# Pooled attention, MLP and experts on one core: weight work in the bursts, high parts of k on GpSimd, transposes around the bursts

## The chip, the cores and the metric

The kernel runs on one core of a Trainium2 chip. The metric is the device time of one execution in microseconds. TensorE (PE in the rows) multiplies matrices, VectorE (DVE) and ScalarE (ACT) work on them element by element, GpSimd (POOL) likewise, and SyncE (SP) issues most loads. Rows write L337 for line 337 of the kernel before; PEld is TensorE loading its stationary operand.

## The reference

```python
# q, k, v: (2, 8, 1152, 64)
q_pool = q.reshape(B, H, S // 2, 2, D).mean(axis=3)
scores = np.matmul(q_pool, k.transpose(0, 1, 3, 2)) / np.sqrt(D)
attn = np.exp(scores - scores.max(-1, keepdims=True))
attn = attn / (attn.sum(-1, keepdims=True) + 1e-09)
x = np.matmul(attn, v)                      # (2, 8, 576, 64) -> (1152, 512)
x = np.maximum(x @ w_in, 0.0) ** 2 @ w_out  # 512 -> 2048 -> 512
# then each token goes to the best of 8 experts, with a capacity:
# out[i] = gate[i] * (relu(x[i] @ w1[e]) @ w2[e])
```

All arrays are float32; the change touches only attention and the preparation of `w_in` and `w_out`, which arrive as 64-bit floats and are narrowed on the chip.

## The kernel before, in words

Products that need more than one pass of reduced precision are made of two parts: a high part (a rounded copy, `fp32r`) and a low part (source minus high part). This holds for q, k, the attention's output x, and the MLP's weights.

**Attention.** A pair is two heads of one batch; there are eight, `p` = 0 to 7. A pair has nine score tiles, so 72 steps: the tile of step n is n itself, the tiles of pair p are 9p to 9p+8. Eight tiles hold 128 pooled queries of one head; the ninth (`h` is None) holds the last 64 of both heads and has twice as many matmuls. `run_step(n)` writes the order of the work by hand. It has the scores of tile n in three pieces (`s_unit`, L337 with k's high part, L339 with its low part; banks sc, two sets in turn), the maximum (`s_max`, VectorE, L344), the exponential (`s_exp`, ScalarE, L349), and the sum's reciprocal of the tile before (`s_rec`, VectorE, L357, L358). Older tiles are transposed (`t_unit`, L372) in three groups: group 0 of tile n-2 into bank bm, copied by ScalarE (L380); group 1 of tile n-2 into bank ba, copied by VectorE (L379), with the reciprocal as its fourth block; group 2 of tile n-3 into the spare columns of the score banks, copied by ScalarE (L380, `late`).

After its tiles are transposed, a pair's tiles meet v in bursts (`burst`, L397): at step 9p+7 the first (u = 0, bank ba), at step 9p+12, which is step 3 of the next pair, the tail (u = 2, bank bm) and then the second (u = 1, bank ba). Behind a burst VectorE scales its two halves (L403), ScalarE makes the high part of x (L407) and GpSimd the low part (L408). In a burst step the order is: scores, maximum, exponential, `late`, reciprocal, burst, extra work, group 0, group 1. In another step: scores, maximum, half of the extra work, group 0, group 1, exponential, `late`, reciprocal, the other half. An engine takes its instructions in this order.

Extra work hangs on steps by `at(n, f)`. The next pair's q halves are added by GpSimd (`q_sum`, L294), scaled by ScalarE (`q_piece`, L299), and the low part is made by VectorE (`q_low`, L304, with a small copy by GpSimd, L308). k comes in three pieces of 384 columns: high part on ScalarE (`k_piece`, L318), low part on GpSimd (L321; for the first pair on VectorE). The first head of a pair does this in the pair's steps 3 to 5, the second in steps 6 to 8 (one later for the first pair), then the loads for the pair after go out on SyncE's queue. On SyncE too are the clearing of two DRAM arrays, the loads of v after each second burst, and those of the MLP's weights.

Five of the sixteen weight blocks of the MLP are prepared in attention, in the order in 0, out 0, in 1, out 1, in 2. A block is loaded and then narrowed by three VectorE instructions of 128x1024 (L169, L175, L181; `narrow_ops` gives the load and the three), at steps 6 to 20, 28 to 36, 39 to 47 and 50 to 58. It is then split: high part on GpSimd (L201, the first two) or ScalarE (L199, the other three), low part on VectorE (L205).

**After attention** follow the MLP, with TensorE matmuls L754 and L780, the choice of experts and the experts' matmuls. The MLP's first matmul follows the last burst.

**Start.** The loads of the first pair go out on SyncE's queue in the order q (first head, 256 columns), k (first head, three pieces), q and k (second head), the rest of q, v. Each load of k is two instructions, one for either half of the partitions.

Of the kernel before, what the change touches and what calls it, by code (L numbers as in the profile page):

```python
# [21 lines left out]
def tile_pooled_attention__relu2_mlp__top1_experts(  # L22
# [14 lines left out]
    nc = tc.nc  # L37
# [105 lines left out]
    wf = {}  # L143
# [132 lines left out]
    def load_k(p, h, c=slice(0, S), eng=nc.sync):  # L276
        b, hp = pairs[p]
        src = k[b, 2 * hp + h][:, c]
        for i in range(2):
            eng.dma_start(out=kqs[h][i * D : (i + 1) * D, c], in_=src)  # L280

    def load_qk(p, h):
        load_q(p, h)
        load_k(p, h)
# [57 lines left out]
    def s_max(n):  # L342
        nm = st[n]["nm"] = sm.tile([P, 1], F32, tag="nm", name="nm", bufs=4)
        nc.vector.tensor_reduce(out=nm, in_=st[n]["S"][:, :, :KS], axis=AX.XY, op=ALU.max, negate=True)  # L344
# [18 lines left out]
    def t_unit(n, i):  # L363
        p, h, j, z = tiles[n]
        bank = (bank_m, bank_a, None)[i]
        if i < 2:
            src = bank.rearrange("p (c n) -> p c n", n=P)
        else:
            src = bank_sets[(n + LAG[2]) % 2][:, :2, KS:]
        for m, c in enumerate(TG[i]):  # L370
            x = st[n]["rc"].to_broadcast([P, P]) if c is None else st[n]["P"][:, c * P : (c + 1) * P]
            nc.tensor.transpose(src[:, m, :], x, ident)  # L372
        blocks = slice(4 * i, 4 * i + len(TG[i]))
        if h is None:
            dst = ptz.rearrange("p c h n -> p c (h n)")[:, blocks, :]
        else:
            dst = pts[:, z, blocks, h, :]
        if i == 1:
            return lambda: nc.vector.tensor_copy(out=dst, in_=src)  # L379
        return lambda: nc.scalar.activation(out=dst, in_=src, func=AF.Copy)  # L380
# [30 lines left out]
        burst(p, 0)  # L411

    def burst1(p):
        burst(p, 2)
        burst(p, 1)
        if p + 1 < NPR:
            load_v(p + 1)

# [7 lines left out]
    for p in range(NPR):  # L426
        big[NT9 * p + 3 + LAG[2] + 1] = lambda p=p: burst0(p)
        big[NT9 * p + 8 + LAG[2] + 1] = lambda p=p: burst1(p)

    def run_step(n):  # L430
        extra = todo.pop(n, [])
        cut = len(extra) // 2
        old = [n - x if 0 <= n - x < N else None for x in LAG]
        late = lambda: None
        if n < N:
            s_unit(n, 0)
            s_unit(n, 1)
        if old[2] is not None:
            late = t_unit(old[2], 2)
        if n < N:  # L440
            s_unit(n, 2)
            s_max(n)
        if n in big:
            if n < N:
                s_exp(n)
            late()
            if 0 < n <= N:
                s_rec(n - 1)
            big[n]()
        for f in extra[:cut]:  # L450
            f()
        for i in range(2):
            if old[i] is not None:
                t_unit(old[i], i)()
        if n not in big:
            if n < N:
                s_exp(n)
            late()
            if 0 < n <= N:
                s_rec(n - 1)  # L460
        for f in extra[cut:]:
            f()

# [1 line left out]
    Q0 = (slice(0, 2 * P), slice(2 * P, SQ))  # L465
    load_q(0, 0, Q0[0])
    for i in range(3):
        load_k(0, 0, slice(i * KS, (i + 1) * KS))
    load_qk(0, 1)
    load_q(0, 0, Q0[1])  # L470
    load_v(0)
    one = const.tile([P, 1], F32, name="one")
# [12 lines left out]
    q_low(0, 0, Q0[0])  # L485
    for i in range(3):
        k_piece(0, 0, i)
    q_sum(1, nc.vector)
    q_piece(0, 1)
    q_low(0, 1)  # L490
    for i in range(3):
        at(0, lambda i=i: k_piece(0, 1, i))
    at(1, lambda: q_sum(0, c=Q0[1]))
    at(2, lambda: q_piece(0, 0, Q0[1]))
    at(2, lambda: q_low(0, 0, Q0[1]))
# [3 lines left out]
    for p in range(NPR - 1):  # L499
        n0 = NT9 * p  # L500
        for h in range(2):
            m = n0 + 2 + 3 * h + (p == 0)
            at(m, lambda h=h: q_sum(h))
            at(m + 1, lambda p=p, h=h: k_piece(p + 1, h, 0))
            at(m + 1, lambda p=p, h=h: q_piece(p + 1, h))
            at(m + 2, lambda p=p, h=h: q_low(p + 1, h))
            for i in (1, 2):
                at(m + 1 + i, lambda p=p, h=h, i=i: k_piece(p + 1, h, i))
            if p + 2 < NPR:
                at(m + 3, lambda p=p, h=h: load_qk(p + 2, h))  # L510

# [1 line left out]
    parts = list(clear_rows())  # L513
    for u in range(len(parts)):
        at(3 + u * 20 // len(parts), lambda: clear_some(parts, 1))
    ops = [f for _ in range(2) for f in nwork.pop(0)]
    for u, f in enumerate(ops):
        at((6, 11, 12, 13, 14, 18, 19, 20)[u], f)
    at(22, lambda: split_hi(("in", 0), wf["in", 0]))
    at(23, lambda: split_lo(("in", 0), wf["in", 0]))  # L520
    at(25, lambda: split_hi(("out", 0), wf["out", 0]))
    at(26, lambda: split_lo(("out", 0), wf["out", 0]))
    for w in range(3):
        for u, f in enumerate(nwork.pop(0)):
            at(28 + 11 * w + (0, 4, 6, 8)[u], f)
    for n, key in ((64, ("in", 1)), (67, ("out", 1)), (N + 1, ("in", 2))):
        at(n, lambda key=key: split_hi(key, wf[key], "act"))
        at(n + 1, lambda key=key: split_lo(key, wf[key]))
    for n in range(N + LAG[2] + 1):
        run_step(n)  # L530
    assert not todo
    att.close()


# [689 lines left out]
```

## Time and profile before

| | us |
|---|---|
| median of 3 runs (lowest to highest) | 663.76 (662.58 to 663.93) |
| profiled execution, its own time | 663.67 |
| its span, first to last instruction | 661.9 |
| TensorE, VectorE, ScalarE, GpSimd busy in the span | 605.4, 362.5, 276.4, 131.3 |
| mean granted clock of TensorE, as a share | 0.984 |

The span is 1.8 us shorter than the execution's time. Busy time is a sum over stages that differ: attention ends at about 299 us. A busy TensorE includes the modelled end of each matmul, which overlaps the next one, so its true idle time is larger than what is left over.

### The profile page before, as it was taken

The page shows a single profiled execution, that of the slowest core. Times are in us where ns is not written, and L with a number is a line of the kernel's source. Part 1 is how long each engine was busy: PE and PEld are TensorE (multiplying, and loading weights), DVE is VectorE, ACT ScalarE, POOL GpSimd, SP SyncE. Part 2 cuts the span into 40 slices and gives each one's busy share as a digit, 9 for nine tenths or more (in the row PEclk, how much of TensorE's full clock was granted, in tenths as well). Part 3 has the DMA queues.
Part 4 walks back from the last instruction along what each step waited for, and adds up shares of the span by engine and source line. Part 5 has one row for each costly group of instructions (what it writes and reads, how often), then busy time and mean ns, then how long its engine had stood idle before and what let it go on. Part 6 is the DMA issues. An engine that isn't in the chain of part 4 may idle for free. (4 is left out here: it accounts for less than half of the span.)

```text
span 661.9 us, 10087 instructions
## 1 busy us (share of the span) xinstructions
PE 605.4 (91%) x3873; PEld 462.5 (70%) x3873; DVE 362.5 (55%) x660; ACT 276.4 (42%) x556; POOL 131.3 (20%) x173
## 2 busy tenths in 40 slices
PE   4998898998899989999999999999999788899994
PEld 2876776777777867769899998998988434444342
DVE  4867777777796867747666688233435311111110
ACT  3765666676767676643232323222343111110110
POOL 3242416141323241001000121000201202000011
PEclk7899999999999999999999999999999989999998
DMA  7795843441625310401223348400100499299800
GB/s 192 192 279 178 261 154 91 112 126 43 189 55 158 86 37 1 164 1 65 64 75 125 119 175 283 178 1 1 40 1 18 158 352 264 94 390 356 292 8 13
DMA packets 35994, 89.23 MB, mean 135 GB/s; under 512 B 4257, under 2 KB 5157, under 8 KB 35936
## 3 DMA queue, kind: packets, MB, share of 16 engines
q1 hardware_dynamic: 34560, 85.66, 41.2%
q0 software_dynamic: 1376, 2.81, 1.2%
q8 instruction: 35, 0.57, 0.4%
q14 instruction: 23, 0.19, 0.1%
HBM read 78.55 MB, written 11.37 MB: 136 GB/s over the span
## 5 line engine op out<-in xcount | busy, mean ns | idle before, releaser
L754 PE MATMUL bs<-ar 128*128 128x384 f32 x576 | 109.0, 338 | 0.0
L344 DVE TENSOR_REDUCE nm<-sc 128x1 f32<-128x1152 f32 x72 | 97.4, 1353 | 18.7 <-PE sc L339 18.0
L754 PEld LDWEIGHTS bs<-ar 128*128 128x128 f32 x576 | 101.6, 188 | 5.0 <-issue 1.6
L349 ACT ACTIVATE af<-sc,nm 128x1152 f32<-128x1152 f32 x72 | 88.1, 1224 | 37.8 <-DVE nm L344 35.8
L337 PE MATMUL sc<-ar 128*128 128x384 f32 x240 | 91.3, 397 | 11.8 <-ACT af L380 5.5
L780 PE MATMUL bt<-ar 128*128 128x512 f32 x360 | 93.2, 395 | 1.2 <-DVE ar L766 1.2
L339 PE MATMUL sc<-ar 128*128 128x384 f32 x240 | 79.4, 347 | 1.1 <-POOL ar L321 0.4
L780 PEld LDWEIGHTS bt<-ar 128*128 128x128 f32 x360 | 66.3, 188 | 14.0 <-DVE ar L766 2.0
L760 ACT ACTIVATE af<-bs 128x384 f32<-128x384 f32 x48 | 23.6, 492 | 121.3 <-PE bs L754 118.3
L397 PE MATMUL ba<-af 128*64 128x256 f32 x576 | 65.3, 380 | 2.1 <-DVE su L357 1.9
L764 DVE TENSOR_TENSOR af<-af 128x384 f32<-128x384 f32 x48 | 26.7, 556 | 71.0 <-ACT af L760 71.0
L337 PEld LDWEIGHTS sc<-ar 128*128 128x128 f32 x240 | 45.5, 195 | 19.5 <-ACT af L380 11.9
L397 PEld LDWEIGHTS ba<-af 128*64 128x64 f32 x576 | 40.0, 137 | 22.8 <-DVE su L357 3.4
L379 DVE COPY af<-ba 128x512 f32<-128x512 f32 x72 | 49.3, 685 | 8.8 <-PE ba L372 8.1
L372 PE MATMUL ba<-ident,af 128*128 128x128 f32 x216 | 37.6, 283 | 15.6 <-DVE af L403 6.7
L380 ACT ACTIVATE af<-bm 128x512 f32<-128x512 f32 x72 | 42.9, 596 | 21.4 <-PE bm L372 21.3
L339 PEld LDWEIGHTS sc<-ar 128*128 128x128 f32 x240 | 46.4, 195 | 2.8 <-POOL ar L321 1.5
L408 POOL TENSOR_TENSOR ar<-af,ar 128x256 fp32r<-128x256 f32 (+1 forms) x24 | 14.4, 601 | 159.6 <-ACT ar L407 159.6
L321 POOL TENSOR_TENSOR ar<-af,ar 64x384 fp32r<-64x384 f32 x42 | 43.2, 1038 | 12.4 <-ACT ar L318 12.4
L372 PE MATMUL bm<-ident,af 128*128 128x128 f32 x288 | 44.6, 278 | 0.1
L372 PEld LDWEIGHTS bm<-ident,af 128*128 128x128 f32 x288 | 34.8, 142 | 8.4 <-issue 5.8
L372 PEld LDWEIGHTS ba<-ident,af 128*128 128x128 f32 x216 | 24.4, 142 | 23.1 <-DVE af L403 10.3
(184 smaller groups left out, 796.6 us busy)
## 6 DMA issues: line engine op xcount, KB each, us to landing
af<-in_moe_w_dram SPq DMA_DIRECT2D x32, 512.0 KB, 9.3
ar<-in_moe_w_dram SPq DMA_DIRECT2D x32, 512.0 KB, 9.7
af<-in_q_dram SPq DMA_DIRECT2D x30, 288.0 KB, 3.7
af<-in_k_dram SPq DMA_DIRECT2D x30, 288.0 KB, 4.4
af<-in_moe_w_in_dram SPq DMA_DIRECT2D x8, 1024.0 KB, 6.3
af<-in_moe_w_out_dram SPq DMA_DIRECT2D x8, 1024.0 KB, 6.1
disp<-af SPq DMA_DIRECT2D x6, 771.0 KB, 8.1
af<-in_v_dram SPq DMA_DIRECT2D x8, 576.0 KB
```

The costliest lines, as they stand in the source:

```text
L321: (eng or (nc.gpsimd if p else nc.vector)).tensor_tensor(out=kl[:D, c], in0=src[:D], in1=kh[:D, c].bitcast(F32), op=ALU.subtract)
L337: nc.tensor.matmul(ps, lhsT=lhs, rhs=bufs_of(p, h)[0][:, c], start=(m == 0), stop=False)
L339: nc.tensor.matmul(ps, lhsT=lhs, rhs=bufs_of(p, h)[1][:, c], start=False, stop=(m == len(ops) - 1))
L344: nc.vector.tensor_reduce(out=nm, in_=st[n]["S"][:, :, :KS], axis=AX.XY, op=ALU.max, negate=True)
L349: nc.scalar.activation(out=pr.rearrange("p (i s) -> p i s", i=3), in_=st[n]["S"][:, :, :KS], func=AF.Exp, bias=st[n]["nm"], accum_out=su,)
L372: nc.tensor.transpose(src[:, m, :], x, ident)
L379: return lambda: nc.vector.tensor_copy(out=dst, in_=src)
L380: return lambda: nc.scalar.activation(out=dst, in_=src, func=AF.Copy)
L397: nc.tensor.matmul(wide(av[hrows[h]]), lhsT=vs[:, h, c * D : (c + 1) * D], rhs=of(c + (c >= RB), h), start=(c == 0), stop=(c == NKC - 1),)
L754: nc.tensor.matmul(ph[:, :TB], lhsT=w[:, cw], rhs=x[:, d, tb * TB : (tb + 1) * TB], start=(n == 0), stop=(n == 3 * NDC - 1),)
L764: nc.vector.tensor_tensor(out=g, in0=r, in1=r, op=ALU.mult)
L780: nc.tensor.matmul(accs[tb][t], lhsT=g[:, ct], rhs=w[:, cw], start=(f == 0 and n == 0), stop=(f == FH - 1 and n == 2),)
```

## The change

- In a burst step group 0 of the transposes and its copy go ahead of the exponential, and so ahead of the burst. Group 1 is held and runs in the next step, after the second score piece and group 2. In all steps the exponential and `late` now come ahead of the extra work.
- At a pair's second burst step the main part (u = 1) runs first and the tail (u = 2) second.
- The three narrowing instructions of a weight block go one each into three burst steps in a row (`aside`), between the reciprocal and the burst; the block's load goes out three steps ahead of the first. Both parts of all five blocks are split by GpSimd, at steps 18, 32, 64, 67 and 73 (high) and one later (low).
- From the second pair on, k's high part is made by GpSimd. The first pair's stays on ScalarE.
- At the start one half of each load of k goes out on ScalarE's queue. The second head's q and k are worked on in steps 0 and 1 instead of ahead of step 0.

```diff
-            eng.dma_start(out=kqs[h][i * D : (i + 1) * D, c], in_=src)
+            (eng if i else nc.sync).dma_start(out=kqs[h][i * D : (i + 1) * D, c], in_=src)
...
     def burst1(p):
+        burst(p, 1)
         burst(p, 2)
-        burst(p, 1)
...
+    held, aside = [], {}
...
             late = t_unit(old[2], 2)
+        for f in held:
+            f()
+        del held[:]
         if n < N:
             s_unit(n, 2)
             s_max(n)
+        if old[0] is not None:
+            t_unit(old[0], 0)()
+        if n < N:
+            s_exp(n)
+        late()
         if n in big:
-            if n < N:
-                s_exp(n)
-            late()
             if 0 < n <= N:
                 s_rec(n - 1)
+            for f in aside.pop(n, []):
+                f()
             big[n]()
         for f in extra[:cut]:
             f()
-        for i in range(2):
-            if old[i] is not None:
-                t_unit(old[i], i)()
-        if n not in big:
-            if n < N:
-                s_exp(n)
-            late()
-            if 0 < n <= N:
-                s_rec(n - 1)
+        if old[1] is not None:
+            second = lambda: t_unit(old[1], 1)()
+            if n in big:
+                held.append(second)
+            else:
+                second()
+        if n not in big and 0 < n <= N:
+            s_rec(n - 1)
...
-        load_k(0, 0, slice(i * KS, (i + 1) * KS))
-    load_qk(0, 1)
+        load_k(0, 0, slice(i * KS, (i + 1) * KS), nc.scalar)
+    load_q(0, 1)
+    load_k(0, 1, eng=nc.scalar)
...
-    q_sum(1, nc.vector)
-    q_piece(0, 1)
-    q_low(0, 1)
+    at(0, lambda: None)
+    at(0, lambda: [q_sum(1, nc.vector), q_piece(0, 1), q_low(0, 1)])
     for i in range(3):
-        at(0, lambda i=i: k_piece(0, 1, i))
+        at(1, lambda i=i: k_piece(0, 1, i))
...
-            at(m + 1, lambda p=p, h=h: k_piece(p + 1, h, 0))
+            at(m + 1, lambda p=p, h=h: k_piece(p + 1, h, 0, hi=nc.gpsimd))
...
-                at(m + 1 + i, lambda p=p, h=h, i=i: k_piece(p + 1, h, i))
+                at(m + 1 + i, lambda p=p, h=h, i=i: k_piece(p + 1, h, i, hi=nc.gpsimd))
...
-    ops = [f for _ in range(2) for f in nwork.pop(0)]
-    for u, f in enumerate(ops):
-        at((6, 11, 12, 13, 14, 18, 19, 20)[u], f)
-    at(22, lambda: split_hi(("in", 0), wf["in", 0]))
...
-    for w in range(3):
-        for u, f in enumerate(nwork.pop(0)):
-            at(28 + 11 * w + (0, 4, 6, 8)[u], f)
-    for n, key in ((64, ("in", 1)), (67, ("out", 1)), (N + 1, ("in", 2))):
-        at(n, lambda key=key: split_hi(key, wf[key], "act"))
-        at(n + 1, lambda key=key: split_lo(key, wf[key]))
+    when = sorted(big)
+    for w in range(5):
+        key = units[w]
+        ops = nwork.pop(0)
+        at(when[3 * w] - 3, ops[0])
+        for u in range(3):
+            aside.setdefault(when[3 * w + u], []).append(ops[1 + u])
+        n = (when[3 * w + 2] + 2, 0, 64, 67, N + 1)[w] or when[3 * w + 2] + 2
+        at(n, lambda key=key: split_hi(key, wf[key]))
+        at(n + 1, lambda key=key: split_lo(key, wf[key], nc.gpsimd))
```

## Rows read from the trace of the kernel before

**Rows 1.** The stage table: busy time of each engine, with its number of instructions, in stretches of the span that end about where a second burst ends; then the granted clock of TensorE, the share of DMA time and GB/s.

```profile
57.00:94.00 37.00, 31.98 (x262) 25.93 (x260) 28.91 (x50) 23.38 (x47) 11.62 (x13) 1.00 0.64 194
94.00:130.00 36.00, 31.43 (x257) 25.29 (x255) 26.32 (x46) 23.50 (x47) 13.83 (x15) 1.00 0.40 113
...
166.00:200.00 34.00, 30.97 (x255) 25.17 (x254) 27.27 (x47) 23.48 (x47) 11.29 (x13) 1.00 0.41 119
200.00:234.00 34.00, 31.80 (x263) 25.75 (x260) 24.73 (x46) 23.39 (x47) 10.85 (x13) 1.00 0.43 119
234.00:270.00 36.00, 32.49 (x262) 26.07 (x262) 25.77 (x47) 24.21 (x48) 10.27 (x12) 1.00 0.05 17
...
299.00:500.00 201.00, 199.80 (x1045) 178.77 (x1046) 117.42 (x185) 62.09 (x123) 18.56 (x21) 1.00 0.27 93
```

**Rows 2.** The waits of TensorE from 17 to 299 us (the waiting instruction's bank and line, what it waited for: us in total, times, longest), and one of VectorE's waits in the same stretch.

```profile
PE ba L372 <- DVE af L403: 6.7, 15, 0.5
PE sc L337 <- ACT af L380: 5.5, 14, 0.4
PE ba L372 <- DVE af L379: 4.8, 9, 1.6
PE sc L337 <- ACT af L349: 4.8, 1, 4.8
PE ba L372 <- DVE su L357: 4.0, 7, 1.0
PE ba L397 <- DVE su L357: 1.9, 2, 1.7
PE bm L397 <- ACT af L380: 1.5, 3, 0.7
PE sc L339 <- POOL ar L321: 0.4, 1, 0.4
...
DVE af L403 <- PE ba L397: 39.0, 15, 3.3
```

**Rows 3.** TensorE in order of time in the pair from 200 to 234 us: start, length, what it is, and in brackets the idle time before it.

```profile
201.84 0.42 PE L337 MATMUL sc<-ar 128*128 128x384 f32 x1
...
202.76 0.42 PE L337 MATMUL sc<-ar 128*128 128x384 f32 x1
...
215.20 0.66 PE L372 MATMUL bm<-ident,af 128*128 128x128 f32 x4
216.31 0.55 PE L372 MATMUL ba<-ident,af 128*128 128x128 f32 x3 [0.46 <-DVE af L403]
...
219.12 0.60 PE L372 MATMUL bm<-ident,af 128*128 128x128 f32 x4
219.56 0.49 PE L372 MATMUL ba<-ident,af 128*128 128x128 f32 x3
...
221.27 0.60 PE L372 MATMUL bm<-ident,af 128*128 128x128 f32 x4
...
222.41 0.44 PE L337 MATMUL sc<-ar 128*128 128x384 f32 x1
```

**Rows 4.** VectorE and ScalarE in order of time in the same pair: two maxima a step apart, the wait for a burst, and a `late` copy.

```profile
206.63 1.34 DVE L344 TENSOR_REDUCE nm<-sc 128x1 f32<-128x1152 f32 x1
...
208.74 1.36 DVE L344 TENSOR_REDUCE nm<-sc 128x1 f32<-128x1152 f32 x1
...
215.39 0.87 DVE L403 TENSOR_TENSOR af<-ba,af 64x256 f32<-64x256 f32 x2 [2.43 <-PE ba L397]
...
206.07 0.38 ACT L380 ACTIVATE af<-sc 128x256 f32<-128x256 f32 x1
```

**Rows 5.** Groups of instructions by shape: VectorE up to 299 us, GpSimd up to 345 us, ScalarE from 20 to 345 us. After the count: busy us, mean ns of one, idle before.

```profile
L175 DVE SCALAR_TENSOR_TENSOR af<-af 128x1024 uint32<-128x1024 uint32 x5 | 8.5, 1699 | 0.1
L181 DVE SCALAR_TENSOR_TENSOR af<-af 128x1024 uint32<-128x1024 uint32 x5 | 6.0, 1207 | 0.0
...
L321 POOL TENSOR_TENSOR ar<-af,ar 64x384 fp32r<-64x384 f32 x42 | 43.2, 1038 | 12.4 <-ACT ar L318 12.4
L408 POOL TENSOR_TENSOR ar<-af,ar 128x256 fp32r<-128x256 f32 x16 | 11.8, 740 | 72.9 <-ACT ar L407 72.9
L201 POOL TENSOR_SCALAR ar<-af 128x1024 fp32r<-128x1024 f32 x4 | 4.5, 1130 | 14.6 <-PE bs L754 10.4 <-DVE af L181 4.2
L308 POOL TENSOR_SCALAR ar<-ar 128x64 fp32r<-128x64 f32 x16 | 3.9, 244 | 32.1 <-DVE ar L304 32.1
...
L318 ACT ACTIVATE ar<-af 128x384 fp32r<-128x384 f32 x42 | 20.4, 520 | 0.0
L349 ACT ACTIVATE af<-sc,nm 128x1152 f32<-128x1152 f32 x71 | 86.9, 1224 | 37.2 <-DVE nm L344 35.2 <-DVE su L357 1.0
```

**Rows 6.** GpSimd and VectorE at the same time, in order of time.

```profile
59.07 1.01 POOL L321 TENSOR_TENSOR ar<-af,ar 64x384 fp32r<-64x384 f32 x1
59.31 1.85 DVE L175 SCALAR_TENSOR_TENSOR af<-af 128x1024 uint32<-128x1024 uint32 x1
```

**Rows 7.** The start in order of time: SyncE's issues of the first k, and TensorE's first scores of the third and the fourth tile.

```profile
2.16 3.80 SPq L280 DMA_DIRECT2D af<-in_k_dram  x6
...
16.52 0.69 PE L337 MATMUL sc<-ar 128*128 128x384 f32 x1 [4.79 <-ACT af L349]
...
20.60 0.69 PE L337 MATMUL sc<-ar 128*128 128x384 f32 x1
```

More of the change, by code (lines that the diff above doesn't have):

```diff
@@ L515, in tile_pooled_attention__relu2_mlp__top1_experts @@
         at(3 + u * 20 // len(parts), lambda: clear_some(parts, 1))
-    ops = [f for _ in range(2) for f in nwork.pop(0)]
-    for u, f in enumerate(ops):
-        at((6, 11, 12, 13, 14, 18, 19, 20)[u], f)
-    at(22, lambda: split_hi(("in", 0), wf["in", 0]))
-    at(23, lambda: split_lo(("in", 0), wf["in", 0]))
-    at(25, lambda: split_hi(("out", 0), wf["out", 0]))
-    at(26, lambda: split_lo(("out", 0), wf["out", 0]))
-    for w in range(3):
-        for u, f in enumerate(nwork.pop(0)):
-            at(28 + 11 * w + (0, 4, 6, 8)[u], f)
-    for n, key in ((64, ("in", 1)), (67, ("out", 1)), (N + 1, ("in", 2))):
-        at(n, lambda key=key: split_hi(key, wf[key], "act"))
-        at(n + 1, lambda key=key: split_lo(key, wf[key]))
+    when = sorted(big)
[8 more added lines that the diff above has]
+        at(n + 1, lambda key=key: split_lo(key, wf[key], nc.gpsimd))
     for n in range(N + LAG[2] + 1):
         run_step(n)
-    assert not todo
+    assert not todo and not aside and not held
     att.close()
```

## The prediction

> **What bounds the kernel now.** I read the stage table first (the busy time of each engine per stretch), then TensorE's waits, then TensorE and VectorE in order of time over one pair of heads, and last the groups by shape. The stage table [rows 1] cuts the attention stage at the ends of its second bursts: a pair takes 34 to 37 us, of which TensorE is busy 31 to 32.5, at the full granted clock (1.00, the 2.4 GHz level). From 299 to 500 us TensorE is busy 199.8 of 201 us, so the MLP starts the moment attention ends and has no gaps: what attention gives up moves the end of the program one for one. All of the change lies in attention and ahead of it.
>
> Attention alternates score steps with two bursts of 4 to 5 us per pair. In a step without a burst VectorE is as full as TensorE: a maximum, a copy and the two small sum instructions, 206.63 to 208.74, 2.11 us [rows 4], while TensorE comes to the same place of the next step 2.15 us later (219.12 to 221.27 [rows 3]). Anything else that VectorE gets in such a step stalls TensorE. In a burst VectorE stands idle: 39.0 us over 15 waits for the burst's products [rows 2], 2.6 us in the mean, 3.3 the longest; the wait of 2.43 us at 215.39 is one [rows 4].
>
> TensorE's waits between 17 and 299 us [rows 2], without the single 4.8 us (that is the start), come to 6.7 + 5.5 + 4.8 + 4.0 + 1.9 + 1.5 + 0.4 = 24.8 us over 51 waits. Each costs more than its idle time, because the matrix pipeline drains. Without a wait the second group of transposes starts 0.44 us after the first (219.12 to 219.56); with an idle time of 0.46 us it starts 1.11 us after (215.20 to 216.31) [rows 3]. So a wait costs its idle time plus 0.21 us; all 51 cost 24.8 + 10.7 = 35.5 us. That is the whole stake of the steady part.
>
> **The change, part by part.**
>
> *First transposes ahead of the burst, second ones held to the next step.* Nothing is added: the same transposes and copies run. The second group writes bank ba, which the burst also fills, so today it waits after each burst for VectorE's two products (15 waits, L403). Held back, it follows two thirds of the next scores and two transposes, 0.92 us of TensorE work (201.84 to 202.76 [rows 3]). The products end about 1.0 us after the burst (0.87 from 215.39 [rows 4], whose burst ended by 215.20 [rows 3]), so after the first burst of a pair, with the handing over, some 0.15 us may remain, seven times; after the second nothing does, since its tail part now runs last and covers the products. Gain: 15 x 0.67 - 1.0 = 9.0 us. Putting the tail part last also gives its operands' copy the time of the main part: the three waits bm L397 on L380 go, 1.5 + 3 x 0.21 = 2.1 us. The price is a step with two copies on VectorE behind a burst: copy about 0.6, products 0.87, the low half of q about 0.75 behind a pair's first burst, all before the next scores are complete, 1.9 to 2.9 us after the burst; I take nothing, and up to 0.3 us for each of 16 as its other bound (4.8 us).
>
> *Weights narrow in bursts.* Fifteen VectorE instructions (three to a weight block; the second kind takes 1.70 us on average here, the third 1.21 [rows 5]) go one by one into the 2.6 us that VectorE waits in a burst. Five subtractions for low parts leave VectorE (one of them after the last score step), three copies leave ScalarE. Waits that end on the queue behind such an instruction are those named su L357 (4.0 us, 7; and 1.9 us, 2, ahead of bursts) and the longest on L379, 1.6 us. Gone: 5.9 + 9 x 0.21 = 7.8, and 1.8: 9.6 us. The remaining eight L379 waits (about 0.45 us) come behind the low half of q, which stays where it is: they stay. The cover for the moved instruction is the burst; if it ran past, the products would be late by the excess, and a burst of some 4 us less about 1.4 that the maximum and the sums still take of it leaves 2.6 us, more than any of the three.
>
> *High parts of k on GpSimd.* 42 ScalarE instructions of 0.52 us [rows 5] become GpSimd ones of 128x384. GpSimd's scalar operation takes 0.24 us at 64 and 1.13 us at 1024 columns [rows 5]; between them 384 gives 0.54 us, an estimate; the two-input subtraction of 64x384, 1.04 us, is the upper bound, and the 0.24 us row the lower. On ScalarE they stood ahead of the copy and the exponential; what waits for that chain is the next use of the score bank, sc L337 on L380: 5.5 us, 14 waits, 8.4 with the drain. A step's chain (scores, maximum, exponential, late copy) is 4.6 us long (201.84 to 206.45 [rows 3, 4]) against two steps of 2.15, so the ones ahead of the first burst, delayed by the low half of q, stay: half goes, 4.2 us (bounds 0 and 8.4). On GpSimd the work is hidden if it ends in time. The tightest place is the pair's second head behind the first burst: the split of the burst's result (0.74) ends about 2.4 us after the burst, then come 0.24, 0.54 + 1.04 and 0.54 + 1.04 [rows 5], 5.8 us after it. The third step after the burst reads them; in the least disturbed pair it starts 7.2 us after the burst (215.20 to 222.41 [rows 3]), by my sum 6.0, and the last piece's low part is read 1.1 us later. Slack 1.2 us. For the first pair everything is a step later, with no slack: I charge 0.5 us. The next loads of k wait on SyncE's queue for GpSimd's subtraction, half a microsecond to two later than now, and what is queued behind them too; they are issued some seven steps ahead of use, 15 us or more, which hides that. The five weight splits, about 1.1 + 2.8 us each (the second, an estimate, is the 64x384 row scaled to 1024 columns), fall in steps 18, 32, 64, 67 and 73, the last three with no k left to split.
>
> GpSimd and VectorE disturb each other. A subtraction on GpSimd ran from 59.07 to 60.08 when a weight instruction began on VectorE at 59.31; that took 1.85 us, 0.64 more than the 1.21 of the like one, as if it began only at 59.95 [rows 5, 6]. This agrees with the Trainium skill, SBUF — State Buffer, section Who interferes with whom: a VectorE instruction with two SBUF inputs and a GpSimd one that reads SBUF lock each other out for a whole instruction. By that rule GpSimd's added reads would stall VectorE, and VectorE GpSimd, by more than the sum has, as in the third rival below.
>
> *First loads on two queues.* SyncE issues six pieces of k in 3.80 us, 0.63 each [rows 7]; three of them go to ScalarE's queue, so the last piece is issued some 2 us earlier. ScalarE's own four issues, 2.5 us at the same price, run before its first work has its data. Today the work on the second head's q stands ahead of the first maximum on VectorE; moved behind, that leaves tile 0 to run at once. But then the second head's k waits on ScalarE for the exponential of tile 1. Worked on from the last piece of k at 6.5 us, an estimate (two issue times earlier by two queues and half by the transfers): scores complete at 8.3; maximum 1.35, exponential with its sum 1.4, q's copy 0.7 and low half 0.75, maximum 1.35, exponential 1.4 [rows 4, 5], high part 0.52: the third tile's scores start at 15.9 instead of 16.52 and the fourth's at 19.6 to 20.0 instead of 20.60 [rows 7]. Gain 1.0 us; bounds 0 and 2.5. The Trainium skill, DMA: Bandwidth & Descriptors, section Issuing engines are not separate DMA queues, grants two queues only the issue time; by that the gain would be the same.
>
> *End of attention.* The last weight split leaves VectorE and ScalarE: 0.5 us.
>
> Sum: 9.0 + 2.1 + 9.6 + 4.2 + 1.0 + 0.5 - 0.5 = 25.9 us. The profiled execution took 663.67 us (span 661.9); the median of the runs is 663.76. Predicted: 663.7 - 25.9 = 637.8 us.
>
> **The rivals.**
>
> *The waits come back.* The four-link chain of a step stays longer than two steps, so removed stalls reappear on the next use of the score bank. For it: the 4.6 us above; against it: bursts let the chain catch up twice per pair. Then pairs would run no faster than the least disturbed ones do, 34 us: of the six whole pairs, two take that and the others 37, 36, 36 and 36 (of the second 36 the row is left out) [rows 1], so 3 + 2 + 2 + 2 = 9 us, with 2 to 3 for the ends 652 us.
>
> *More than the sum.* All waits go, also those behind the low half of q: 35.5 + 1.5 = 37, 627 us. Against it: that half stays in the same place.
>
> *GpSimd locked out.* Each high part takes 1.04 us and meets one lock of 0.64 us (the delay at 59.31): the chain behind the first burst grows by 2 x (0.5 + 0.6) = 2.2, 1.0 past its slack, on seven pairs: 7 us back, 645 us. For it: one of TensorE's waits was already on GpSimd, 0.4 us [rows 2].
>
> *Slower than before.* The same chain, long enough to eat all: 25.9 / 7 = 3.7 us per pair beyond the 1.2 of slack, so each of the two high parts 2.45 us longer, 3.0 us instead of 0.54; beyond that it decides, and at 4 us each the time would be 663.7 - 25.9 + 7 x 5.7 = 678 us. No GpSimd row of this size comes near.
>
> **How the numbers follow.** Forecast (631 to 645 us) 0.62; waits come back (645 to 657) 0.17; GpSimd locked out (643 to 652) 0.08; more than the sum (624 to 631) 0.09; slower 0.04. The range from 627 to 653 takes in the unknown costs and leaves out about 0.15 to 0.2. A difference under 0.2% (1.3 us) is about what a measurement here can't tell from none: faster 0.94, same 0.02, slower 0.04.
>
> **What would show it.** Right: no wait of ba L372 on L403; none on su L357 outside the start; ScalarE without 128x384 copies after the first pair; second bursts 31.5 to 33 us apart; VectorE's idle time at the products down by some 15 us. Wrong: new waits of the score matmuls on GpSimd in the third step behind first bursts; GpSimd high parts over 1 us; waits on L380 growing past 5.5 us; the MLP starting no earlier than 290 us instead of about 273.

## The result, and the profile after

The changed kernel takes 646.12 us (median of 4, 644.73 to 646.86) where the kernel before takes 663.85 beside it (median of 4, 662.58 to 664.2): ratio 0.9734, 95% interval 0.9713 to 0.9755, 17.7 us faster. Forecast were 25.9 us, 637.8. The cleanest measure of the parts is the start of the MLP's first matmul, since all of the change lies ahead of it: it moved from 298.93 to 280.57 us, by 18.36; the forecast put it at about 273. What lies behind it took 363.0 us of the span before and 364.0 after, and between 360.3 and 363.7 in the runs below, so a difference of up to some 4 us in the total time says little about one part.

TensorE from 86 to 119 us, from 151 to 183 and in the first 201 us of the MLP, as in the stage table of before (busy us of TensorE, its weight loads, VectorE, ScalarE, GpSimd, each with its count; granted clock, DMA share, GB/s):

```profile
86.00:119.00 33.00, 31.86 (x265) 26.54 (x263) 25.38 (x48) 21.83 (x44) 13.79 (x19) 1.00 0.49 140
151.00:183.00 32.00, 30.85 (x258) 25.73 (x257) 25.32 (x46) 20.82 (x42) 13.77 (x19) 1.00 0.44 116
281.00:482.00 201.00, 199.81 (x1048) 178.98 (x1047) 118.02 (x190) 61.75 (x124) 21.26 (x22) 1.00 0.27 93
```

A pair that took 34 to 37 us [rows 1] now takes 32.3: the second bursts of the first seven pairs start at 54.43, 86.74, 119.05, 151.39, 183.72, 216.03 and 248.37. ScalarE has lost some 2 us a pair and GpSimd has gained some 3; the clock stays at its upper level, and the MLP is as full as before.

TensorE's waits of the changed kernel from its first burst (35.6) to the end of attention (281): the waiting instruction, its releaser, us in total, times, longest.

```profile
PE sc L337 <- ACT af L380: 3.7, 12, 0.4
PE ba L372 <- DVE af L379: 3.2, 8, 0.4
PE sc L339 <- POOL ar L321: 0.6, 1, 0.6
PE ba L397 <- DVE af L379: 0.6, 1, 0.6
PE ba L372 <- DVE af L403: 0.3, 1, 0.3
PE sc L372 <- ACT af L380: 0.3, 1, 0.3
```

That is 8.7 us in 24 waits, where before had 24.9 in 51 between the same two places ([rows 2] without the ones ahead of 33 us, and with one of 0.3 us that rows 2 leave out). The waits behind a weight instruction (su L357) and those of the tail burst (bm) are gone, and those on the products (L403) but for one, as forecast. The two largest of the list are not: the next scores still wait for the copy of the transposes (L380, 5.5 in 14 before), and transposes wait for VectorE's copy (L379, 4.6 in 8).

VectorE's wait for the products in the same kernel, from 17 to 281 us, and its waits for the weights' loads:

```profile
DVE af L403 <- PE ba L397: 26.2, 14, 4.3
...
DVE af L169 <- DMA af<-in_moe_w_in_dram: 3.1, 1, 3.1
DVE af L169 <- DMA af<-in_moe_w_out_dram: 2.4, 2, 2.2
```

39.0 us [rows 2] have become 26.2, 12.8 less where the forecast's sign was some 15. Not all of the 12.8 us is work: three of the narrowing instructions now wait in a burst for their weight block, 5.5 us together, where before had no such wait. Mostly the burst's matmuls hide that. But in the first burst the instruction starts at 40.28, the burst ends at 39.67, and the products behind it are what TensorE waits for in the one wait on L403 that is left (0.3 us; 1.0 in best, whose first burst is earlier). In u_khigh, below, such a load costs more.

The start is later, not earlier. TensorE of the changed kernel, the third tile's first scores and the first burst, and between them two waits:

```profile
17.81 0.69 PE L337 MATMUL sc<-ar 128*128 128x384 f32 x1 [5.38 <-ACT ar L318]
...
31.52 0.66 PE L372 MATMUL bm<-ident,af 128*128 128x128 f32 x4 [0.58 <-ACT af L380]
33.22 0.55 PE L372 MATMUL ba<-ident,af 128*128 128x128 f32 x3 [1.04 <-DVE af L379]
...
35.04 0.60 PE L372 MATMUL bm<-ident,af 128*128 128x128 f32 x4
35.56 4.11 PE L397 MATMUL ba<-af 128*64 128x256 f32 x36
```

Before, that burst began at 32.98:

```profile
32.98 4.11 PE L397 MATMUL ba<-af 128*64 128x256 f32 x36 [0.26 <-DVE su L357]
```

Of the 2.58 us, 0.52 are only a change of place (the first transposes of the step, 35.04 to 35.56, now stand ahead of the burst); 2.06 are lost. The third tile's scores came at 16.52 before [rows 7], were forecast at 15.9, and come at 17.81.

So the 18.36 us are made of 20.42 gained behind the first burst (24.9 forecast) and 2.06 lost ahead of it (1.0 gain forecast). These two shortfalls, 4.5 and 3.1 us, are what the experiments were for.

### The profile page after: what moved, and what is told of

It reads as the page before. It is cut to its first block, busy times and chain, and to the rows that moved or that the text cites. A ratio compares the mean times of both kernels' runs of the same rounds, so it can differ in the third digit from the quotient of the medians.

```text
span 644.6 us, 10110 instructions
## 1 busy us (share of the span) xinstructions
PE 602.3 (93%) x3873; PEld 465.2 (72%) x3873; DVE 356.3 (55%) x655; ACT 257.2 (40%) x511; POOL 162.6 (25%) x223
## 5 line engine op out<-in xcount | busy, mean ns | idle before, releaser
L769 DVE TENSOR_TENSOR af<-af 128x384 f32<-128x384 f32 x48 | 28.4, 591 | 72.3 <-ACT af L765 72.3
L379 DVE COPY af<-ba 128x512 f32<-128x512 f32 x72 | 49.3, 685 | 14.5 <-PE ba L372 14.3
L380 ACT ACTIVATE af<-bm 128x512 f32<-128x512 f32 x72 | 43.0, 597 | 25.5 <-PE bm L372 25.5
L372 PE MATMUL bm<-ident,af 128*128 128x128 f32 x288 | 43.7, 275 | 0.7 <-ACT af L380 0.6
L201 POOL TENSOR_SCALAR ar<-af 128x1024 fp32r<-128x1024 f32 x15 | 21.2, 1414 | 89.2 <-DVE af L175 54.7
L321 POOL TENSOR_TENSOR ar<-af,ar 64x384 fp32r<-64x384 f32 x42 | 41.9, 998 | 3.5
L372 PE MATMUL ba<-ident,af 128*128 128x128 f32 x216 | 36.6, 278 | 4.6 <-DVE af L379 4.3
L372 PEld LDWEIGHTS bm<-ident,af 128*128 128x128 f32 x288 | 36.1, 142 | 3.8 <-ACT af L380 1.4
```

The source lines that it names most:

```text
L321: (eng or (nc.gpsimd if p else nc.vector)).tensor_tensor(out=kl[:D, c], in0=src[:D], in1=kh[:D, c].bitcast(F32), op=ALU.subtract)
L769: nc.vector.tensor_tensor(out=g, in0=r, in1=r, op=ALU.mult)
```

## The experiments

Each row is a kernel; its ratio is to the kernel before, run beside it. The last two columns are from its profiled execution.

| kernel | what it is | us | ratio, 95% interval | first burst | MLP starts |
|---|---|---|---|---|---|
| before | | 663.85 | | 32.98 | 298.93 |
| after | | 646.12 | 0.9734 (0.9713 to 0.9755) | 35.56 | 280.57 |
| u_start | after, with the start of before | 644.65 | 0.9718 (0.969 to 0.9745) | 34.84 | 280.33 |
| u_queue | after, all loads on SyncE | 643.88 | 0.9696 (0.9672 to 0.9719) | 34.83 | 279.99 |
| u_khigh | after, high parts of k on ScalarE | 651.08 | 0.9819 (0.9789 to 0.9848) | 35.00 | 285.74 |
| u_narrow | after, weight work where it was | 657.13 | 0.9895 (0.986 to 0.9931) | 38.07 | 295.47 |
| u_turn | after, order of a step as it was | 653.96 | 0.9856 (0.983 to 0.9881) | 32.71 | 286.87 |
| late_first | after, `late()` ahead of the exponential | 654.98 | 0.9863 (0.9837 to 0.9889) | 36.40 | 290.43 |
| q_aside | after, low half of q inside bursts | 638.97 | 0.9624 (0.9595 to 0.9653) | 35.54 | 276.07 |
| combo | u_queue, late_first and q_aside | 653.86 | 0.986 (0.9822 to 0.9898) | 35.66 | 288.33 |
| b_narrow | before, weight work alone changed | 652.81 | 0.9829 (0.9811 to 0.9847) | 32.15 | 289.60 |
| b_turn | before, order of a step alone changed | 661.32 | 0.996 (0.9931 to 0.999) | 34.40 | 296.80 |
| b_khigh | before, high parts of k alone moved | 666.51 | 1.0032 (1.0017 to 1.0047) | 32.82 | 302.53 |
| best | after, SyncE's loads, low half of q in bursts, old order in the first steps | 637.69 | 0.9604 (0.9588 to 0.962) | 32.34 | 273.49 |

### The start: u_start and u_queue

u_start puts back the loads of before and the second head's q work ahead of the first step; u_queue puts back only the loads:

```diff
-            (eng if i else nc.sync).dma_start(out=kqs[h][i * D : (i + 1) * D, c], in_=src)
+            eng.dma_start(out=kqs[h][i * D : (i + 1) * D, c], in_=src)
...
-        load_k(0, 0, slice(i * KS, (i + 1) * KS), nc.scalar)
-    load_q(0, 1)
-    load_k(0, 1, eng=nc.scalar)
+        load_k(0, 0, slice(i * KS, (i + 1) * KS))
+    load_qk(0, 1)
```

> The changed kernel with the start of the kernel before: all first loads on SyncE's queue, the second head's q ahead of the first maximum. Theory A (the start of the changed kernel costs time, since the k loads on ScalarE's queue share the transfers with the first 256 columns of q: these land at 5.83 us instead of 4.32, and the first burst begins at 35.56 instead of 32.98): the undone start gives 2 to 3 us back, about 643.5, first burst near 33. Rival (the first burst is late for work inside the steps, not for the start): 646, first burst near 35.5.

> The changed kernel with all loads on SyncE's queue again; the second head's work stays in steps 0 and 1. If the second queue alone makes the start late: 643 to 644, the first 256 columns of q landing near 4.3 us, first burst near 33. If the moved work on the second head makes it late: 646, first burst near 35.

Both start the first burst 0.7 us earlier than the changed kernel (34.84, 34.83), not near the 33 that was expected, and the MLP 0.2 and 0.6 us earlier. The second queue is therefore a loss, and the place of the second head's q work makes no difference at the burst. Why the queue loses is seen at the first q, on VectorE and on the two queues, in the changed kernel:

```profile
0.80 1.50 SPq L274 DMA_DIRECT2D af<-in_q_dram  x2
0.81 2.52 ACTq L280 DMA_DIRECT2D af<-in_k_dram  x4
...
5.83 0.43 DVE L294 TENSOR_TENSOR af<-af 128x256 f32<-128x256 f32 x1 [3.70 <-DMA af<-in_q_dram]
```

and in u_queue:

```profile
0.80 1.32 SPq L274 DMA_DIRECT2D af<-in_q_dram  x2
2.16 3.80 SPq L280 DMA_DIRECT2D af<-in_k_dram  x6
4.30 0.43 DVE L294 TENSOR_TENSOR af<-af 128x256 f32<-128x256 f32 x1 [2.17 <-DMA af<-in_q_dram]
```

The q pieces are issued at the same time in both, but with k's pieces beside them from 0.81 us on, q lands 1.5 us later. It is so in every kernel here: the addition starts between 5.48 and 6.68 us in the six with two queues, and between 4.30 and 4.49 in the others. The forecast had counted issue times and half a transfer time, and had not asked which load the first instruction waits for. The trace agrees here with the Trainium skill, DMA: Bandwidth & Descriptors, section Issuing engines are not separate DMA queues, in more than the saved issue time: transfers of all queues run on the same 16 engines and interleave. Read so, a piece issued early on a second queue takes from the one that is needed first.

This is 0.73 of the 2.06 us. The rest shows in u_turn and best, below.

### One part undone at a time: u_khigh, u_narrow, u_turn

u_khigh takes `hi=nc.gpsimd` out of both calls of `k_piece`; u_narrow puts the weight schedule of before in place of the block from `when = sorted(big)` on; u_turn puts back `run_step` of before (with the narrowing kept in the burst) and the tail burst ahead of the main one:

```diff
-                at(m + 1 + i, lambda p=p, h=h, i=i: k_piece(p + 1, h, i, hi=nc.gpsimd))
+                at(m + 1 + i, lambda p=p, h=h, i=i: k_piece(p + 1, h, i))
```

> The changed kernel with k's high parts on ScalarE as before. Theory A (the move to GpSimd was worth the 4.2 us of the sum): 650. Theory B (the score bank's chain still sets the step, since maximum, exponential and late copy are unchanged, and ScalarE had room): 646 to 647, with the waits of L337 on L380 unchanged near 4 us.

> The changed kernel with the weights' narrowing and splitting at the steps and on the engines of the kernel before. Theory A (worth the 9.6 us of the sum): 655 to 656, waits on L357 back. Rival (with the transposes moved, the queue on VectorE has room for it): 648 to 650.

> The changed kernel with the order inside the steps and of the second burst as before; the weight work stays in the bursts. Theory A (the moved transposes were worth the 11.1 us of the sum): 657, 15 waits on L403 back. Theory B (part of it reappears in the next steps' waits on the score bank, whichever order): 651 to 654.

By the start of the MLP, undoing costs 5.2 us (k high), 14.9 (weights) and 6.3 (order). With the start's -0.2 that is 26.1 us, more than the 18.4 that all have brought together: a part is worth more when the others are in place, so these prices can't be added up. By time, u_khigh came out as its theory A said, but with waits nearer to theory B; u_narrow 1 us past its theory A; u_turn as theory B.

*k high.* The waits that the forecast wanted to shorten with it are the same without it. u_khigh from its first burst to the end of attention:

```profile
PE sc L337 <- ACT af L380: 2.6, 6, 0.4
PE ba L372 <- DVE af L403: 1.7, 2, 1.4
PE sc L337 <- ACT ar L318: 1.5, 1, 1.5
```

Six waits of 0.4 us on L380, one to a pair, stand in both kernels; the changed one has six of 0.2 more. Per pair the high parts on ScalarE cost only 0.34 us (155.52 to 188.19 between second bursts is 32.67; the changed kernel's 32.33). The rest of what u_khigh loses is in the first pair (2.0 us from first to second burst, with the 1.5 us above for a high part that came late on ScalarE) and in one event, which cost 1.6 us: a weight load landed late and held a narrowing instruction in a burst, and the products behind it (the 1.4 us). That load is late because of the edit. In u_khigh:

```profile
81.99 1.01 POOL L321 TENSOR_TENSOR ar<-af,ar 64x384 fp32r<-64x384 f32 x1 [3.09 <-ACT ar L318]
...
83.03 1.11 SPq L280 DMA_DIRECT2D af<-in_k_dram  x2
...
84.81 0.49 SPq L160 DMA_DIRECT2D af<-in_moe_w_out_dram  x1
...
94.71 0.69 DVE L169 TENSOR_SCALAR af<-af 128x1024 uint32<-128x1024 uint32 x1 [4.79 <-DMA af<-in_moe_w_out_dram]
```

The next load of k waits for GpSimd's last subtraction, which waits for the high part on ScalarE, and the weight load stands behind it on SyncE's queue. In the changed kernel that subtraction ends at 79.61, the load goes out at 81.42, and the narrowing starts at 90.30, just inside a burst that runs from 86.74 to 90.85.

*Weights.* u_narrow has back what the forecast named, waits behind weight instructions, here from 17 to 295 us:

```profile
PE ba L372 <- DVE af L379: 5.9, 12, 1.0
PE sc L337 <- ACT af L380: 5.8, 18, 0.4
...
PE ba L372 <- DVE su L357: 3.9, 4, 1.8
PE ba L397 <- DVE su L357: 1.9, 3, 1.3
```

5.8 us in 7 waits on su L357, and more and longer ones on the two copies. Of its 14.9 us, 2.5 lie ahead of the first burst (38.07): 0.6 at the third tile's scores (18.43 against 17.81), and the rest's cause stays open; the other 12.4 stand against the forecast's 9.6 + 0.5 for the part.

*Order.* u_turn has the waits on the products back, 8.1 us in 15 (6.7 in 15 before [rows 2]). But its first burst starts at 32.71, 2.85 us ahead of the changed kernel's:

```profile
14.71 0.66 PE L337 MATMUL sc<-ar 128*128 128x384 f32 x1 [2.33 <-ACT ar L318]
...
32.71 4.11 PE L397 MATMUL ba<-af 128*64 128x256 f32 x36 [0.26 <-DVE su L357]
```

Less the 0.52 of change of place, 2.3 us, with the two queues kept. The new order of a step puts the exponential ahead of `extra`, and in the first steps `extra` is the second head's k: its high part waits on ScalarE behind the exponential of the tile before, and the third tile's scores come at 17.81 instead of 14.71. That is the larger part of the lost start, and it belongs to the order, not to the loads: behind the first burst the order is worth 6.3 + 2.3 = 8.6 us here. The 2.3 and the queue's 0.73 are more than the 2.06 that were lost in all, so other parts of the change gain some 1 us ahead of the first burst; b_narrow, below, has that burst 0.83 us earlier than before.

### One part alone on the kernel before: b_narrow, b_turn, b_khigh

> The kernel before with the weight work alone changed: narrowing in the bursts, all splits on GpSimd. By the sum: 9.6 us faster plus 0.5 at the end, 653.5. If the parts share their waits, so that whichever comes first earns more: up to the 15 us that undoing it cost in the changed kernel's attention stage, 649 to 651.

> The kernel before with the order of the transposes and of the second burst alone changed. By the sum: 11.1 us faster, 652.5. By the undoing in the changed kernel (8.6 us behind the first burst, 2.3 lost ahead of it): 657. If waits on L403 turn into waits behind the weight work, which still stands in the plain steps: 658 to 662.

> The kernel before with k's high parts alone on GpSimd. By the sum: 4.2 us faster, 659.5. If the weight work on VectorE hides what ScalarE gives up: 662 to 664. If GpSimd and VectorE hold each other up more (weight work and low halves against twice the GpSimd work): slower, 665 or more.

Alone, the weights bring 9.3 us at the start of the MLP, near the forecast's 9.6 + 0.5; the order brings 2.1 (its first burst comes 1.42 us later than before, so 3.0 behind it without the 0.52 of change of place); and the high parts of k cost 3.6: b_khigh is slower than before, by 0.17 to 0.47%. The order alone clears the waits on the products, and b_turn gets in their place, from 17 to 297 us,

```profile
PE ba L372 <- DVE su L357: 6.0, 6, 1.3
```

where before had 4.0 in 7 [rows 2]: a TensorE that comes earlier waits longer behind the same weight instructions. That is only a part of what the order did not bring; with the waits of bursts on su L357 it is 6.7 us in 8, against 5.9 in 9. And b_khigh shows what GpSimd's new work does to weight instructions that stand in plain steps, and they to it:

```profile
59.07 0.51 POOL L320 TENSOR_SCALAR ar<-af 128x384 fp32r<-128x384 f32 x1
59.31 1.34 DVE L175 SCALAR_TENSOR_TENSOR af<-af 128x1024 uint32<-128x1024 uint32 x1
59.66 1.85 POOL L321 TENSOR_TENSOR ar<-af,ar 64x384 fp32r<-64x384 f32 x1
...
63.66 0.99 POOL L321 TENSOR_TENSOR ar<-af,ar 64x384 fp32r<-64x384 f32 x1
63.72 2.02 DVE L181 SCALAR_TENSOR_TENSOR af<-af 128x1024 uint32<-128x1024 uint32 x1
64.63 1.48 POOL L320 TENSOR_SCALAR ar<-af 128x384 fp32r<-128x384 f32 x1
```

At 59.66 the subtraction takes 1.85 us instead of 1.0, until about one such length after VectorE's instruction ends (60.65); at 63.72 VectorE takes 2.02 instead of the 1.2 it takes undisturbed [rows 5], and the next high part 1.48 instead of 0.51. With them TensorE's waits on su L357 are 8.5 us in 8 (5.9 in 9 before). So what the rival "GpSimd locked out" describes does happen. Whether the edit gains or loses doesn't hang on the weights alone, though. Two more pairs of kernels differ only in the high parts and in the start, which costs 0.2 us by u_start: u_narrow starts the MLP 1.3 us ahead of b_turn, with the weights in plain steps and the new order, and u_turn 2.7 us ahead of b_narrow, with the weights in bursts and the old order. The edit loses, 3.6 us, only where the old order and weights in plain steps come together.

### What keeps the remaining waits: late_first and q_aside

Two causes were left for the waits on L380: the length of a step's chain (scores, maximum, exponential, copies), and the low half of q, which runs on VectorE between a maximum and a copy. late_first changes the chain, q_aside moves the low half of q (from the second pair on) ahead of a burst's matmuls in VectorE's and TensorE's order, where the weights are, and with the first head's low half its scaled copy on ScalarE (`q_piece`):

```diff
+        late()
         if old[0] is not None:
             t_unit(old[0], 0)()
         if n < N:
             s_exp(n)
-        late()
```

```diff
+            elif h == 0:
+                aside.setdefault(m + 1, []).append(lambda p=p, h=h: q_piece(p + 1, h))
+                aside.setdefault(m + 1, []).append(lambda p=p, h=h: q_low(p + 1, h))
+            else:
+                at(m + 1, lambda p=p, h=h: q_piece(p + 1, h))
+                aside.setdefault(m + 2, []).append(lambda p=p, h=h: q_low(p + 1, h))
```

> The changed kernel with the late copy (group 2 of the transposes) ahead of group 0's copy and the exponential on ScalarE, so that the next use of a score bank waits for the exponential alone. Theory B (the chain scores, maximum, exponential, late copy of 4.6 us against two steps of 2.15 is what still paces the steps): the chain loses 0.3 us, three waits per pair shrink, 640 to 642, pairs of 31.4 us instead of 32.3. Rival (VectorE's order paces them): 645 to 646.

> The changed kernel with the low half of q made ahead of the burst matmuls, in the burst step, instead of in the step behind a second burst (the first pair excepted). If the wait of L372 on L379 in the second step behind a second burst (0.41 us and its drain) and the wait on L380 one step later come from the low half of q, both go: 1.2 us for each of six pairs, 638 to 640. If the chain alone sets them: 645 to 646.

> The last three together: loads on SyncE's queue, late copy first, low half of q in the burst step. If they add up: 646 less 2.5, 5 and 7, about 632; if the low half of q and the chain are one and the same stall: 636 to 639.

q_aside settles the second. From its first burst to the end of attention:

```profile
PE sc L337 <- ACT af L380: 1.2, 6, 0.2
PE ba L372 <- DVE af L379: 0.8, 2, 0.4
```

3.7 in 12 and 3.2 in 8 have come down to 1.2 in 6 and 0.8 in 2: the six waits of 0.4 on L380 and six of the eight on L379 are gone. A pair takes 31.54 us (second bursts at 149.38 and 180.92), 0.8 less than in the changed kernel, and the MLP starts 4.5 us earlier, not the 7.2 of the expectation. That the total time meets it (7.15 us less than the changed kernel) is luck: in the profiled executions 2.4 us of it come from the stretch behind the MLP's start, which the edit doesn't touch. How the low half of q makes both waits is seen in the changed kernel, VectorE and then TensorE from 158 to 166 us:

```profile
158.74 1.35 DVE L344 TENSOR_REDUCE nm<-sc 128x1 f32<-128x1152 f32 x1
160.12 0.76 DVE L304 SCALAR_TENSOR_TENSOR ar<-af,ar 64x576 fp32r<-64x576 f32 x1
160.91 0.69 DVE L379 COPY af<-ba 128x512 f32<-128x512 f32 x1
...
161.66 0.55 PE L372 MATMUL ba<-ident,af 128*128 128x128 f32 x3 [0.41 <-DVE af L379]
164.97 0.44 PE L337 MATMUL sc<-ar 128*128 128x384 f32 x1 [0.42 <-ACT af L380]
```

The copy begins 0.76 us late, TensorE waits 0.41 for it; everything behind that on VectorE, the next maxima too, keeps the delay, and with them the exponential and the copy on ScalarE: the wait at 164.97 is, read so, the same 0.4 us come round a second time, and q_aside, in which both are gone together, bears that out. The scaled copy that q_aside moved as well is not in the way here: in the changed kernel it runs on ScalarE at 157.32 for 0.67 us, and ScalarE then stands idle for 0.66 us ahead of the exponential at 160.18, waiting for the maximum.

late_first was to shorten the chain and made it longer. ScalarE in that kernel:

```profile
164.67 0.39 ACT L380 ACTIVATE af<-sc 128x256 f32<-128x256 f32 x1 [2.14 <-DVE nm L344]
164.95 0.59 ACT L380 ACTIVATE af<-bm 128x512 f32<-128x512 f32 x1
165.43 1.22 ACT L349 ACTIVATE af<-sc,nm 128x1152 f32<-128x1152 f32 x1
```

The late copy (`af<-sc`), put ahead of the exponential, doesn't start in the time when ScalarE stands idle but waits 2.14 us for the maximum (163.29 to about 164.64), so two copies, 0.76 us, now stand between maximum and exponential where none stood. A pair takes 33.6 us (155.94 to 189.54), 1.3 more, with new waits bm L372 on L380, 9.5 us in 32 from 17 us on. Neither of its theories came. So a longer chain does cost; that a shorter one would gain was not shown. Why that copy waits for the maximum was not settled: `late` transposes go into a free part of a score bank, and the trace only names the releaser. combo holds the same edit, loses the same way and misses both of its theories.

### All together: best

best is the changed kernel with SyncE's loads (u_queue), the low half of q in bursts (q_aside) and, in the first seven steps, `extra` ahead of the exponential again:

```diff
             s_max(n)
+        if n < 7:
+            for f in extra[:cut]:
+                f()
+            extra, cut = extra[cut:], 0
```

and one empty entry, `at(1, lambda: None)`, so that all three pieces of k fall into the part that comes first.

> The changed kernel with all loads on SyncE's queue, the low half of q in the burst step, and for the first seven steps the extra work ahead of the exponential as before. Theory (the start loses 0.7 us to the second queue and 2.3 us to extra work behind the exponential, and the low half of q loses 1.2 us in each of six pairs): first burst at 32.5 to 33.5, 635 to 637. If the low half's gain depends on the later start: 638 to 640.

It takes 637.69 us, 4.0% less than before (3.8 to 4.1) and some 8 less than the changed kernel. TensorE's start:

```profile
14.64 0.69 PE L337 MATMUL sc<-ar 128*128 128x384 f32 x1 [3.34 <-ACT ar L318]
...
32.34 4.11 PE L397 MATMUL ba<-af 128*64 128x256 f32 x36
```

The first burst starts 3.22 us earlier than in the changed kernel and the MLP 7.08. Of the 3.22, u_queue has 0.73, and q_aside moves that burst by 0.02 only, so the other 2.5 are the order of the first seven steps: the third tile's scores come at 14.64 where u_queue has them at 17.11, 2.5 us as well. The two causes of the late start and the low half of q thus come to the 7.5 us that were missing, to within half a microsecond; but the low half is a gain that the forecast had left out ("they stay"), not one that it had counted. That the total comes to the forecast 637.8 is a coincidence of the terms, not a proof of them: the kernel is another.

## Why the prediction was right, and which steps were off

The mechanism held: full steps, empty bursts, work moved from the one to the other, and attention's end moves the program's. Direction and range held; the size was 8 us too good, and inside it one term was paid by another mechanism than the one named. Step by step, the waits between first burst and the end of attention in both kernels, at the 0.21 us of drain for each:

| step | forecast, us | from the waits | |
|---|---|---|---|
| order: products (L403) and tail (bm) | 9.0 + 2.1 | 8.2 in 18 to 0.3 in 1: 11.5 | right |
| weights: su L357 | 7.8 | 5.9 in 9 to 0: 7.8 | right |
| weights: longest of L379 | 1.8 | 4.6 in 8 to 3.8 in 9: 0.6 | too large |
| k high: half of L380 | 4.2 | 5.5 in 14 to 3.7 in 12: 2.2 | wrong cause |
| first pair, GpSimd late | -0.5 | -0.2 | right |
| end of attention | 0.5 | no wait of its own | open |
| start | +1.0 | -2.06 | wrong sign |

- *Order and weights in bursts* (11.1 and 7.8) are right to half a microsecond in the whole kernel: no wait on su L357 is left, and one on L403. The runs add that what a part brings depends on which others are there: the order brings 2.1 us alone on the kernel before, and 6.3 where the other parts are in place. The forecast's prices of the order and the weights hold for all edits at once only.
- *"so the ones ahead of the first burst, delayed by the low half of q, stay: half goes, 4.2 us."* The step that failed is who pays for the half that goes. Of the 14 waits of 0.3 to 0.4 us on L380, the ones ahead of a first burst stay, six of 0.4, and q_aside shows the low half of q behind them, as forecast. The other half went. But it is gone in u_khigh too, with the high parts on ScalarE (2.6 us in 6), so it was not the high parts that made it; with them on GpSimd six new waits of 0.2 us stand there instead. Undone, the high parts are worth 5.2 us by other ways: 0.34 us in each of six pairs, about 2 us in the first pair, where the forecast charged 0.5, and 1.6 by the late weight load, less 0.6 ahead of the first burst. That this is near the 4.2 is luck.
- *The start.* "Gain 1.0 us" failed. The sum had the wait of the second head's k for the exponential in it. From the first tile's maximum to the third tile's scores it puts 7.5 us (8.3 + 7.5 is 15.8, not 15.9), and they took 7.3, from 10.55 to 17.81. Its start failed: "worked on from the last piece of k at 6.5 us", scores complete at 8.3. The changed kernel works on that piece at about 8.5 us, and its first maximum starts at 10.55; u_queue, with one queue, has 7.96 and 9.85. So the second queue brought no piece of that head's k earlier and cost 0.7 us, and the earlier start that was to pay for the exponential did not come. TensorE's first score pieces also take 0.66 to 0.69 us each in the changed kernel, from 7.30 on, and 0.45 before, from 5.93 on; what that adds was not separated.
- *Sum of the steady part.* The waits give 21.9 us, the measured times of the same stretch 20.4 (20.94, less the 0.52 of change of place). The 1.5 us between lie in gaps that no wait names, and their cause stays open.
- *GpSimd.* The estimate for the high part, 0.54 us, measured 0.51, and no score matmul waits for GpSimd but once (0.6 us, first pair). Against the rival of the locked-out GpSimd the forecast was right for the changed kernel; b_khigh shows that it depends on the other edits. The second instruction of a weight split was put at 2.8 us and takes 2.0:

```profile
L320 POOL TENSOR_SCALAR ar<-af 128x384 fp32r<-128x384 f32 x42 | 21.4, 509 | 0.0
L205 POOL TENSOR_TENSOR ar<-af,ar 128x1024 fp32r<-128x1024 f32 x5 | 10.0, 1998 | 0.3
```

- *The rivals.* Waits that come back (652) did so in part: the six 0.2 us waits on L380 are new ones. Pairs run at 32.3 us, not at 34. "More than the sum" (627): best has the waits behind the low half of q gone too and still takes 637.69.

## What to carry to other kernels

When an engine waits behind several small instructions, undo and add each edit separately, and look in the trace at which waits go, before giving it the waits: here one 0.76 us instruction on VectorE made two waits of TensorE, 3.3 us apart, and the second named ScalarE, whose own work had not grown. What one part brings alone need not be what it brings among the others, not even in sign: test it in both places. An order that is right for the steady state can be wrong for the first steps, where work that is otherwise a filler is what the next tile needs; price the two stretches separately. Before first loads are spread over two queues, ask which load the first instruction waits for, and keep that one alone.

## What the runs showed of the hardware that was not expected

- GpSimd and VectorE hold each other up both ways, by amounts as large as the instructions: GpSimd's subtraction took 1.85 instead of 1.0 us beside a weight instruction, its 128x384 scalar operation 1.48 instead of 0.51, and a weight instruction 2.02 instead of 1.2 (b_khigh). The same 42 operations moved to GpSimd cost 3.6 us in the kernel before and bring 5.2 in the changed one.
- Moved out of the plain steps, the second weight instruction takes 1.21 us, where it averaged 1.70 [rows 5]. The row is of the changed kernel up to 299 us; five of the eight stand in bursts, three behind attention:

```profile
L175 DVE SCALAR_TENSOR_TENSOR af<-af 128x1024 uint32<-128x1024 uint32 x8 | 9.7, 1214 | 0.1
```

- Pieces of k on a second queue at 0.81 us moved the landing of a q piece, issued at 0.80 us on the first queue, from 4.3 to 5.8 us (5.48 to 6.68 in the six kernels that have them).
